# R mixture's scalings from VectorE to GpSimd, and the fourth group's convolution with its matmuls ahead of its casts

## The chip, the cores and the metric

One core of one Trainium2 chip. The time is the device time of one execution, in microseconds (us); a quoted time is the median of several executions. Kernels that are compared ran alternately on the same chip.

## The reference, cut to what matters

`x` is [8, 4160, 192]. First a causal convolution over seven positions with softmax weights for each of 8 heads, then a channel mixture:

```python
x_prev = shift(x, one position)
xk = mu_k * x + (1 - mu_k) * x_prev
xr = mu_r * x + (1 - mu_r) * x_prev
k = maximum(xk @ w_k, 0)              # 192 -> 1024
v = k * k @ w_v                       # 1024 -> 192
out = sigmoid(xr @ w_r) * v
```

## The kernel before

The kernel takes pairs of batches in steps of 512 positions, 34 in all, and writes `xk = x_prev + mu_k * d` with `d = x - x_prev`. A step of ordinary length takes two *rounds* (the code calls them bundles) of TensorE work; each round has 24 K matmuls, 12 R and 32 V, and often some of the convolution of a later group. ScalarE makes relu and sigmoid and the casts of the convolution; VectorE makes the differences, both mixtures, the squares and the product with the sigmoid (`o_sb`). GpSimd issues the loads of x, which cast fp32 to bf16 on the way.

```python
def diff(s, ...):                      # d = y[1:] - y[:-1], three thirds of the channels at once
    nc.vector.tensor_tensor(out=diffs[s], in0=y_of(s, cs, 1), in1=y_of(s, cs, 0), op=ALU.subtract)

def mix(s, i, ...):                    # i = 0: K mixture, i = 1: R mixture
    d = diffs[s]
    t = two.tile([P, NC, STEP], BF16, tag=("xk", "xr")[i])        # two buffers
    ...
    for c in range(sl.start, sl.stop):                            # three scalings of 128x512
        nc.vector.tensor_scalar(out=t[:, c, :L], in0=d[:, c, :L], scalar1=mu[:, i, c : c + 1], ...)
    nc.vector.tensor_tensor(out=o, in0=o, in1=y_of(s, sl, 0), op=ALU.add)
```

The order in which the instructions are written down, for each round `b`:

```python
run(early, b)        # x tile (with a tiny VectorE write into it) and x loads on GpSimd
k_section(ns); k_relu(n) ...; run(rq, b)      # K matmuls, relus, R matmuls
run(vq, b)           # V matmuls
run(mixes, b)        # D round: diff and K mixture of the next step. R round: R mixture
k_square(n) x3; run(vo, b)  # o_sb
run(xt, b); k_square(n); run(late, b)
```

The K, R, V and convolution results share a ring of four PSUM tiles.

## Time and profile before

| | before |
|---|---|
| time | 434.81 us (433.78 to 435.53, 3 runs) |
| TensorE, VectorE, ScalarE, GpSimd busy | 97, 87, 80, 14% |
| a round with and without a convolution | 6.27 and 5.94 us |
| one bf16 scaling of 128x512 on VectorE | 0.35 us |

How to read it: nothing but TensorE is full. What another engine does can cost time only where TensorE comes to wait for it; so one looks not at busy shares but at how late a VectorE result may be before a matmul wants it, and in which of the two rounds.

### The profile page before, as it was taken

The numbers are of one execution on the slowest core, as the hardware profiler recorded it, in microseconds if no ns is written. First come the engines' busy times: TensorE is split into PE (matmuls) and PEld (weight loads), VectorE is DVE, ScalarE is ACT, GpSimd is POOL, SyncE is SP. The second block draws the span as 40 slices with busy tenths as digits, with TensorE's granted clock in tenths as the row PEclk, the third lists the DMA queues.
The fourth block names the chain that finished last, engine by engine and source line by source line (L and its number), as shares of the span: only waits on it lengthen the run. The fifth ranks groups of instructions, "written<-read, shape, count | busy, mean of one in ns | idle before, by whom it ended". The sixth has DMA issues, their size and how long they took to land.

```text
span 433.3 us, 12070 instructions
## 1 busy us (share of the span) xinstructions
PE 419.2 (97%) x5045; PEld 293.3 (68%) x5045; DVE 377.2 (87%) x678; ACT 348.0 (80%) x427; POOL 62.5 (14%) x101
## 2 busy tenths in 40 slices
PE   6879999999999999999999999999999999999995
PEld 3447677667767766776677667766766776667785
DVE  5859978888988899888889989888898889999983
ACT  5776989888988888888889878988898887777780
POOL 6651002123210200303030200203000000000000
PEclk9989999999999999999999999999999999999999
DMA  7998694999996976589796994496847484311223
GB/s 126 192 160 127 166 191 106 195 210 196 193 195 166 177 196 124 87 199 158 181 194 158 175 214 111 96 225 128 185 110 143 119 204 87 111 65 48 74 75 109
DMA packets 136444, 64.73 MB, mean 149 GB/s; under 512 B 87122, under 2 KB 136006, under 8 KB 136390
## 3 DMA queue, kind: packets, MB, share of 16 engines
q1 hardware_dynamic: 96536, 48.29, 47.2%
q0 software_dynamic: 38960, 15.08, 30.2%
q8 instruction: 39, 0.64, 0.6%
q10 hardware_dynamic: 894, 0.61, 0.5%
q14 instruction: 15, 0.12, 0.1%
HBM read 30.75 MB, written 36.96 MB: 156 GB/s over the span
## 4 chain that ended last, share of the span: by engine, by line
PE 90%; ACT 4%; DMA 2%; issue 2%; POOL 1%; DVE 0%; ACTq 0%
PE ps_v L576 41%; PE ps_k L519 38%; PE ps_r L593 7%; PE ps_c L321 4%; ACT k_sb L548 3%; DMA wk<-in_moe_w_k_dram 2%; ACT y L384 1%; POOL xb L155 0%; ACT y L351 0%; PE ps_c L342 0%; PE ps_t L419 0%; ACT r_sb L601 0%; PE ps_c L366 0%; POOL wk L214 0%; DVE x_f L720 0%
## 5 line engine op out<-in xcount | busy, mean ns | idle before, releaser
L548 ACT ACTIVATE k_sb<-ps_k 128x1024 bf16<-128x1024 f32 x260 | 246.1, 1043 | 22.7 <-PE ps_k L519 22.4
L519 PE MATMUL ps_k<-xk,wk 64*128 64x512 bf16 (+1 forms) x1632 | 182.0, 369 | 2.1 <-ACT k_sb L548 1.2
L576 PE MATMUL ps_v<-wv,k 128*128 128x192 bf16 x2080 | 182.7, 246 | 0.9 <-ACT k_sb L548 0.9
L576 PEld LDWEIGHTS <-k 128*128 128x128 bf16 x2080 | 168.7, 98 | 10.9 <-issue 10.9
L562 DVE TENSOR_TENSOR k<-k_sb 128x1024 bf16<-128x1024 bf16 x260 | 167.1, 684 | 0.4 <-ACT k_sb L548 0.4
L519 PEld LDWEIGHTS <-wk 64*128 64x128 bf16 x1632 | 75.0, 94 | 89.1 <-issue 11.4
L617 DVE TENSOR_TENSOR o_sb<-ps_v,r_sb 128x768 f32<-128x768 f32 x64 | 61.2, 956 | 35.5 <-PE ps_v L576 31.7
L384 ACT CAST y<-ps_c 128x960 bf16<-128x960 f32 (+7 forms) x81 | 50.7, 668 | 45.4 <-PE ps_c L321 45.4
L134 POOL DMA_DIRECT2D xb<-in_x_dram x56 | 40.3, 732 | 205.5 <-PE ps_k L519 158.8
L601 ACT ACTIVATE r_sb<-ps_r 128x768 bf16<-128x768 f32 x65 | 55.7, 857 | 1.3 <-PE ps_r L593 1.3
L593 PEld LDWEIGHTS <-xr 64*128 64x128 bf16 x780 | 34.0, 94 | 16.3 <-DVE xb L112 1.3
L593 PE MATMUL ps_r<-wr,xr 64*128 64x192 bf16 x780 | 42.9, 243 | 0.9 <-DVE xb L112 0.8
L499 DVE TENSOR_TENSOR xr<-xr,yT 128x1536 bf16<-128x1536 bf16 (+1 forms) x33 | 31.0, 939 | 1.1
L472 DVE TENSOR_TENSOR d<-yT 128x1536 bf16<-128x1536 bf16 (+2 forms) x35 | 31.1, 887 | 0.8 <-DMA yT<-y_dram 0.7
L499 DVE TENSOR_TENSOR xk<-xk,yT 128x1536 bf16<-128x1536 bf16 (+1 forms) x32 | 30.4, 950 | 1.1
L495 DVE TENSOR_SCALAR xk<-d,mu 128x512 bf16<-128x512 bf16 (+1 forms) x99 | 30.3, 361 | 1.2
L495 DVE TENSOR_SCALAR xr<-d,mu 128x512 bf16<-128x512 bf16 (+1 forms) x102 | 29.3, 343 | 0.0
L321 PE MATMUL ps_c<-xb,toe 64*64 64x240 bf16 (+1 forms) x448 | 20.0, 265 | 0.0
L321 PEld LDWEIGHTS <-toe 64*64 64x64 bf16 x448 | 8.3, 105 | 7.7 <-issue 7.7
L456 POOL COPY y_tail<-yT 128x195 bf16<-128x195 bf16 x4 | 1.6, 398 | 69.6 <-DMA yT<-y_dram 69.6
L428 DVE COPY yT<-ps_t 128x720 bf16<-128x720 bf16 (+1 forms) x7 | 3.2, 500 | 6.7 <-PE ps_t L419 6.7
L131 POOL DMA_DIRECT2D xb<-in_x_dram x14 | 7.6, 544 | 1.4 <-POOL xb L114 0.9
(55 smaller groups left out, 58.5 us busy)
## 6 DMA issues: line engine op xcount, KB each, us to landing
out_dram<-o_sb SPq DMA_DIRECT2D x128, 192.0 KB
xb<-in_x_dram POOLq DMA_DIRECT2D x36, 240.0 KB, 7.3
y_dram<-y SPq DMA_DIRECT2D x22, 360.0 KB
xb<-in_x_dram POOLq DMA_DIRECT2D x10, 216.0 KB, 5.4
y_dram<-y SPq DMA_DIRECT2D x22, 75.0 KB
y_dram<-y SPq DMA_DIRECT2D x6, 216.0 KB
xb<-in_x_dram POOLq DMA_DIRECT2D x6, 144.0 KB, 6.0
xb<-in_x_dram POOLq DMA_DIRECT2D x4, 192.0 KB, 8.0
```

The lines of the kernel that those rows point to most:

```text
L134: nc.gpsimd.dma_start(out=xb[i * Q : (i + 1) * Q, full[0] : full[-1] + 1, s, :], in_=bass.AP(tensor=x.tensor, offset=x.offset + (b * S + b ...
L321: nc.tensor.matmul(out=ps[j * Q : (j + 1) * Q, i, 0 : nb * w].rearrange("p (n s c) -> p n s c", n=nn, s=2)[:, :, :, k * G : (k + 1) * G], ...
L384: copy(out=y[:, :, :, a // Q, :, a % Q : a % Q + b - a], in_=src[:, :, :, :, a - c0 : b - c0])
L495: nc.vector.tensor_scalar(out=t[:, c, :L], in0=d[:, c, :L], scalar1=mu[:, i, c : c + 1], scalar2=None, op0=ALU.mult)
L499: nc.vector.tensor_tensor(out=o, in0=o, in1=y_of(s, sl, 0), op=ALU.add)
L519: nc.tensor.matmul(out=ps[:, i, f * L : (f + 1) * L], lhsT=wk[r, c, fs], rhs=xk[r, c, :L], start=c == 0 and f == 0, stop=c == NC - 1 and f ...
L548: nc.scalar.activation(out=k_sb, in_=ps.rearrange("p a b -> p (a b)"), func=AF.Relu)
L562: nc.vector.tensor_tensor(out=o, in0=i, in1=i, op=ALU.mult)
L576: nc.tensor.matmul(out=o, lhsT=k2s[s][:, f, t * P : (t + 1) * P], rhs=wv[:, f, :], start=(f == 0), stop=(f == NF - 1),)
L593: nc.tensor.matmul(out=ps[:, i, k * D : (k + 1) * D], lhsT=xr[q, c, ts], rhs=wr[q, c, :], start=c == 0, stop=c == NC - 1,)
L601: nc.scalar.activation(out=r_sbs[s, j], in_=ps[:, :, 0 : 2 * D], func=AF.Sigmoid)
L617: nc.vector.tensor_tensor(out=o_sb.rearrange("p (b t) d -> p b (t d)", b=2), in0=v_ps.pop((s, j)), in1=r_sbs.pop((s, j)), op=ALU.mult,)
```

## The change

VectorE is the second busiest engine and GpSimd nearly idle, so from the fourth step on the R mixture's three scalings go there; the add stays. And the fourth group's convolution, whose second bank's matmuls waited for the casts of the first, issues all four matmuls first.

```diff
@@ conv_full
-        for k in range(2):
-            ps = ps2[:, k, 0 : nb * 2 * w].rearrange("p (n s c) -> p n s c", n=nb, s=2)
+        banks = [ps2[:, k, 0 : nb * 2 * w].rearrange("p (n s c) -> p n s c", n=nb, s=2) for k in range(2)]
+        for k, ps in enumerate(banks):
             for i in range(2):
                 ... matmul
+        for k, ps in enumerate(banks):
             ... casts
@@ mix
+        eng = nc.gpsimd if i == 1 and s > 2 else nc.vector
         for c in range(sl.start, sl.stop):
-            nc.vector.tensor_scalar(
+            eng.tensor_scalar(
```

## The prediction

The prediction's time of one GpSimd scaling (0.64 us) and its costs of a collision (0.36 us each; 1.9 to 2.1 us in a D round under the second rival, that of a slower scaling) are my estimates: they rest on rates an element that no run had shown.

> **What bounds the kernel now.** I read the page's busy shares first, then the shares by slice, then the waits that end in a matmul, and last the VectorE and TensorE timelines of one ordinary step.
>
> ```profile
> PE 419.2 (97%) x5045; PEld 293.3 (68%) x5045; DVE 377.2 (87%) x678; ACT 348.0 (80%) x427; POOL 62.5 (14%) x101
> ...
> PE   6879999999999999999999999999999999999995
> ...
> POOL 6651002123210200303030200203000000000000
> ```
>
> TensorE is busy 97% of the span and, after the first 75 us, without a gap that the profile shows. VectorE is at 87%, GpSimd at 14%: that invites the change. But VectorE is not the bound on average; in slices where TensorE is full, freeing VectorE gives nothing by itself.
>
> ```profile
> PE ps_c L342 <- ACT y L351: 2.1, 2, 1.1
> ```
>
> This is the longest entry of TensorE's waits: twice the fourth group's second bank waited for ScalarE's casts of the first. All of TensorE's waits listed there sum to under 10 us, most of it before 25 us.
>
> The VectorE timeline of one step (start, length, instruction; in brackets the idle time before it and what ended it):
>
> ```profile
> 163.74 0.96 DVE L617 TENSOR_TENSOR o_sb<-ps_v,r_sb 128x768 f32<-128x768 f32 x1 [0.79 <-PE ps_v L576]
> 164.62 0.68 DVE L562 TENSOR_TENSOR k<-k_sb 128x1024 bf16<-128x1024 bf16 x1
> 165.22 0.95 DVE L472 TENSOR_TENSOR d<-yT 128x1536 bf16<-128x1536 bf16 x1
> 166.21 0.88 DVE L495 TENSOR_SCALAR xk<-d,mu 128x512 bf16<-128x512 bf16 x3
> 167.12 0.96 DVE L499 TENSOR_TENSOR xk<-xk,yT 128x1536 bf16<-128x1536 bf16 x1
> 168.00 1.89 DVE L562 TENSOR_TENSOR k<-k_sb 128x1024 bf16<-128x1024 bf16 x3
> 170.01 0.96 DVE L617 TENSOR_TENSOR o_sb<-ps_v,r_sb 128x768 f32<-128x768 f32 x1
> 170.88 0.68 DVE L562 TENSOR_TENSOR k<-k_sb 128x1024 bf16<-128x1024 bf16 x1
> 171.48 0.87 DVE L495 TENSOR_SCALAR xr<-d,mu 128x512 bf16<-128x512 bf16 x3
> 172.39 0.96 DVE L499 TENSOR_TENSOR xr<-xr,yT 128x1536 bf16<-128x1536 bf16 x1
> 173.27 1.89 DVE L562 TENSOR_TENSOR k<-k_sb 128x1024 bf16<-128x1024 bf16 x3
> 176.28 0.96 DVE L617 TENSOR_TENSOR o_sb<-ps_v,r_sb 128x768 f32<-128x768 f32 x1 [1.12 <-PE ps_v L576]
> ```
>
> A step is two TensorE rounds of 6.27 us. I call them the D round (o_sb at 163.74 up to the next at 170.01: difference, K scaling) and the R round (170.01 to 176.28, with the three R scalings). The D round is full: from the o_sb at 163.74 nothing idles, and the next one starts 170.01, just as its V matmuls end. The R round has 1.12 us of idle. So VectorE's spare time lies all in the R round, where the scalings are removed, and none in the D round.
>
> ```profile
> 167.16 2.81 PE L576 MATMUL ps_v<-wv,k 128*128 128x192 bf16 x32
> 169.90 0.40 PE L321 MATMUL ps_c<-xb,toe 64*64 64x240 bf16 x8
> 170.24 2.76 PE L519 MATMUL ps_k<-xk,wk 64*128 64x512 bf16 x24
> ```
>
> The PSUM ring has four tiles. The D round's V tile, freed when o_sb ends at 170.97, is taken again four allocations later: a convolution unit, then the third K tile. That K tile starts about half-way in the 24 matmuls, near 171.5. So o_sb may come about 0.57 us later before TensorE waits (about 0.8 us in rounds without a convolution, where the fourth K tile takes it).
>
> [...] The trace of before has one GpSimd operation that reads SBUF beside busy VectorE, the last copy of y_tail:
>
> ```profile
> L456 POOL COPY y_tail<-yT x4: 363/369/493, 107.4 to 370.7; 128x195 bf16<-128x195 bf16 x4
> ```
> ```profile
> 370.32 0.68 DVE L562 TENSOR_TENSOR k<-k_sb 128x1024 bf16<-128x1024 bf16 x1
> 370.92 0.44 DVE L495 TENSOR_SCALAR xr<-d,mu 128x512 bf16<-128x512 bf16 x1
> ```
>
> That copy took 493 ns instead of 363 (it began at 370.72, inside the square), and the scaling behind the square took 0.44 us instead of its usual 0.35. [...] It is one observation, so weak.
>
> **The change part by part.**
>
> *Convolution.* Eight matmuls in two groups of four; the second pair of each no longer waits. It removes at most the 2.1 us of the wait. But ScalarE must still make the same six casts, and a few us later (32 to 37 us) TensorE waits for ScalarE and VectorE (0.23 and 0.37 us). I take half: 1 us gained, once.
>
> *Scalings removed from VectorE.* 31 of the 34 steps, three each: 93 instructions at a pitch of 0.87/3 = 0.29 us, about 27 us of VectorE. They go from the R round, which idled 1.12 us already: idle there becomes about 2 us. On the path: 0.
>
> *Scalings added on GpSimd.* An estimate of one: a copy of 195 elements took 0.363 us[...], together 0.64 us. Three take 1.9 us of a 12.5 us step, and GpSimd has room. The added instruction order shows them released as soon as the difference is written and the R buffer of two steps before is free, not when the R round begins: so they start in the full D round. The add that needs them comes a whole round later, and it won't wait.
>
> *Collision.* The three meet seven VectorE instructions in the D round (three K scalings, add, three squares). What one costs VectorE: the 195-element copy cost about 0.1 us[...], so 0.36 us each, 1.1 us for three. Of that 0.57 us is slack in rounds with a convolution and 0.8 without. Of 31 D rounds 8 have x loads queued on GpSimd just ahead (2.9 us for four), which push the scalings behind most of the round: I count nothing for them. About 15 with a convolution lose 1.1 - 0.57 = 0.53 us each, 8.0 us; about 8 without lose some 0.25 us, 2.0 us. The loss isn't won back: the R round's o_sb waits for the V matmuls that were put off, and the next D round starts from it.
>
> *Sum.* 434.8 - 1 + 10 = 444 us under this theory.
>
> **The rivals.**
>
> [...] If back-to-back VectorE instructions don't let GpSimd in, [...] Nothing stalls, and only the convolution's gain stays: 433 us. Against it speaks the one copy above; for it, that descriptor writing beside squares left nearly all of them at 684 ns[...].
>
> [...] VectorE then loses 1.9 to 2.1 us in the D round: 15 x 1.4 + 8 x 1.2, and some 0.5 in the other 8, is 35 us, near 468 us. Nothing in before's trace shows this operation.
>
> *VectorE relief pays.* If the 27 us counted, the time would fall over 2%. TensorE's gapless rounds of 6.27 us speak against it.
>
> *The x loads come late* behind scalings that wait. The loads run many rounds before their use, so this costs nothing, I think.
>
> **Range and chances.** About half the weight lies on 433 (no collision that shows, or one that fits the slack), a third on 440 to 452, the rest above. I put the point between, at 440 us, and the range at 430 to 461. The limit of 2% is 443.5 us, just where the middle theory lands; so slower by over 2% gets 0.38, within 2% 0.60, and faster 0.02, as no more than some 3 us of removable waiting is to be seen.
>
> **What would show it.** Right, if in the new profile squares and K scalings of VectorE just after a difference are longer than 684 and 346 ns, o_sb of the D round ends over 0.57 us after its V matmuls in excess of before, and K matmuls show waits for o_sb with rounds over 6.27 us. Wrong, if these durations stand as before and TensorE's rounds stay 6.27 us (the first rival), or if one GpSimd scaling's pitch is well over 0.64 us (the second). The convolution is right if the wait for the casts is gone and TensorE is about 1 us ahead at 50 us. All fails if the R add turns out to wait for GpSimd: then my order of release is wrong.

## The result, and the profile after

468.62 us (466.47 to 470.66, 4 runs): slower, with a ratio of 1.0772 (95% interval 1.071 to 1.0834).

From the page of the changed kernel, shares and slices; PEclk is TensorE's granted clock in tenths:

```profile
PE 430.6 (92%) x5045; PEld 301.4 (64%) x5045; DVE 374.2 (80%) x585; ACT 348.5 (74%) x427; POOL 232.0 (50%) x194
...
PE   7789999797798999997799999999599999999996
...
PEclk9989999999799999999799999999899999999999
```

TensorE is no longer gapless: there are three deep dips, near 115, 222 and 335 us, and the clock falls at each (to 7, 7 and 8 tenths in those slices). VectorE's busy time hardly falls (377.2 to 374.2), although 27 us of scalings left it: what remained got longer. GpSimd gained 170 us. The costliest groups show from what:

```profile
L497 POOL TENSOR_SCALAR xr<-d,mu 128x512 bf16<-128x512 bf16 (+1 forms) x93 | 169.4, 1833 | 127.5 <-DVE d L473 84.3
...
L501 DVE TENSOR_TENSOR xr<-xr,yT 128x1536 bf16<-128x1536 bf16 (+1 forms) x33 | 31.4, 952 | 45.4 <-POOL xr L497 45.3
```

One scaling takes 1833 ns on average, not 640, and the R add now waits 45 us for them. The waits say how this gets to TensorE (engine, line, what it waited for: total, times, longest):

```profile
DVE xr L501 <- POOL xr L497: 45.3, 11, 9.8
...
PE ps_k L521 <- ACT k_sb L550: 16.9, 4, 5.8
ACT k_sb L550 <- DVE k L564: 15.5, 3, 5.7
...
PE ps_k L521 <- DVE o_sb L619: 6.7, 12, 1.7
```

The R add stands in VectorE's queue ahead of three squares. While it waits they wait, ScalarE then has no free buffer for its relu, and TensorE no free PSUM tile. One of the three dips, GpSimd's timeline, then VectorE's and TensorE's:

```profile
107.83 0.70 POOL L134 DMA_DIRECT2D xb<-in_x_dram  x1 [12.27 <-issue]
...
110.94 0.71 POOL L134 DMA_DIRECT2D xb<-in_x_dram  x1
111.68 4.65 POOL L497 TENSOR_SCALAR xr<-d,mu 128x512 bf16<-128x512 bf16 x3
```
```profile
100.92 0.95 DVE L473 TENSOR_TENSOR d<-yT 128x1536 bf16<-128x1536 bf16 x1
...
107.22 0.06 DVE L112 MEMSET xb<- 1x1 uint32 x1
116.36 0.96 DVE L501 TENSOR_TENSOR xr<-xr,yT 128x1536 bf16<-128x1536 bf16 x1 [9.09 <-POOL xr L497]
```
```profile
112.21 2.12 PE L521 MATMUL ps_k<-xk,wk 64*128 64x512 bf16 x18
119.10 1.46 PE L521 MATMUL ps_k<-xk,wk 64*128 64x512 bf16 x6 [4.77 <-ACT k_sb L550]
...
121.45 3.65 PE L578 MATMUL ps_v<-wv,k 128*128 128x192 bf16 x32
```

The difference was there at 101.87. GpSimd sat idle before 107.83: next in its queue stood not the scalings but x loads of the same round, and those waited for the tiny VectorE write at 107.22. (So the program has it; the profile's `issue` names no releaser. In all three dips the loads begin 0.6 to 1.3 us after this write.) Then came 3.8 us of loads and 4.65 us of scalings, and the add started at 116.36. After the stall the V matmuls take 3.65 us instead of 2.81: TensorE's clock is 0.50 from 119 to 123 us by the view of stretches.

The distances from one set of V matmuls to the next, kernel against kernel, give a balance, in us. The three dips: 6.05 + 1.89, 7.09 + 1.14, 6.43 + 1.14, together 23.7 (some 0.9 of it in the step of a single round behind the first dip, which experiments 3, 4, 9 and 10 keep). The rounds from each D round with x loads on, three to each: 9.5. A stretch of low clock at 31 us: 1.6. All other rounds together: 1.6. Less 1.7 for an earlier first V, this is 34.8 us before rounding.

Of the 9.5, 1.9 us are not a wait for GpSimd: in one round, at 87 us, the difference waits for the transposing load that brings the convolution's output. Experiment 10, which has that step's scalings back on VectorE, keeps this wait (2.0 us), and experiment 4, with its x loads later, has none. What lengthens it was not tested.

An ordinary D round, VectorE's timeline of the changed kernel:

```profile
181.18 1.31 DVE L497 TENSOR_SCALAR xk<-d,mu 128x512 bf16<-128x512 bf16 x3
...
183.41 2.30 DVE L564 TENSOR_TENSOR k<-k_sb 128x1024 bf16<-128x1024 bf16 x3
185.63 0.95 DVE L619 TENSOR_TENSOR o_sb<-ps_v,r_sb 128x768 f32<-128x768 f32 x1
```

The predicted collision is there: 1.31 instead of 0.88 and 2.30 instead of 1.89, together 0.84 us. But it isn't where most of the 34 us went.

### The profile page after: what moved, and what is told of

It reads as the page before. It is cut to its first block, busy times and chain, and to the rows that moved or that the text cites. A ratio compares the mean times of both kernels' runs of the same rounds, so it can differ in the third digit from the quotient of the medians.

```text
span 468.0 us, 12099 instructions
## 1 busy us (share of the span) xinstructions
PE 430.6 (92%) x5045; PEld 301.4 (64%) x5045; DVE 374.2 (80%) x585; ACT 348.5 (74%) x427; POOL 232.0 (50%) x194
## 5 line engine op out<-in xcount | busy, mean ns | idle before, releaser
L497 POOL TENSOR_SCALAR xr<-d,mu 128x512 bf16<-128x512 bf16 (+1 forms) x93 | 169.4, 1833 | 127.5 <-DVE d L473 84.3
L521 PE MATMUL ps_k<-xk,wk 64*128 64x512 bf16 (+1 forms) x1632 | 187.5, 370 | 26.7 <-ACT k_sb L550 16.9
L578 PE MATMUL ps_v<-wv,k 128*128 128x192 bf16 x2080 | 186.4, 249 | 1.3 <-ACT k_sb L550 1.3
L564 DVE TENSOR_TENSOR k<-k_sb 128x1024 bf16<-128x1024 bf16 x260 | 178.7, 727 | 1.5 <-ACT k_sb L550 1.4
L578 PEld LDWEIGHTS <-k 128*128 128x128 bf16 x2080 | 171.9, 99 | 12.2 <-issue 11.8
L521 PEld LDWEIGHTS <-wk 64*128 64x128 bf16 x1632 | 77.2, 94 | 115.6 <-issue 41.4
L501 DVE TENSOR_TENSOR xr<-xr,yT 128x1536 bf16<-128x1536 bf16 (+1 forms) x33 | 31.4, 952 | 45.4 <-POOL xr L497 45.3
L595 PEld LDWEIGHTS <-xr 64*128 64x128 bf16 x780 | 36.3, 96 | 17.7 <-issue 3.9
L497 DVE TENSOR_SCALAR xk<-d,mu 128x512 bf16<-128x512 bf16 (+1 forms) x99 | 39.5, 454 | 1.2
L501 DVE TENSOR_TENSOR xk<-xk,yT 128x1536 bf16<-128x1536 bf16 (+1 forms) x32 | 32.6, 1018 | 1.1
L715 PE MATMUL warm<-zeros,ones_t 128*128 128x512 bf16 x16 | 6.3, 577 | 1.8 <-DVE zeros L730 1.8
```

Of the source, the lines that this page charges most:

```text
L497: eng.tensor_scalar(out=t[:, c, :L], in0=d[:, c, :L], scalar1=mu[:, i, c : c + 1], scalar2=None, op0=ALU.mult)
L521: nc.tensor.matmul(out=ps[:, i, f * L : (f + 1) * L], lhsT=wk[r, c, fs], rhs=xk[r, c, :L], start=c == 0 and f == 0, stop=c == NC - 1 and f ...
L564: nc.vector.tensor_tensor(out=o, in0=i, in1=i, op=ALU.mult)
L578: nc.tensor.matmul(out=o, lhsT=k2s[s][:, f, t * P : (t + 1) * P], rhs=wv[:, f, :], start=(f == 0), stop=(f == NF - 1),)
L595: nc.tensor.matmul(out=ps[:, i, k * D : (k + 1) * D], lhsT=xr[q, c, ts], rhs=wr[q, c, :], start=c == 0, stop=c == NC - 1,)
```

## The experiments

The first theory is that of the **queue**: GpSimd's scalings take so long, and stand behind x loads in so many steps, that the R add waits. The second is the prediction's, that of the **collision**: in each D round VectorE loses time to the GpSimd scalings that run beside it (the 0.84 us just seen). Each diff is against the changed kernel, unless it says otherwise.

**1. The convolution alone.**

```diff
-        eng = nc.gpsimd if i == 1 and s > 2 else nc.vector
+        eng = nc.vector
```

> The convolution part alone, all scalings on VectorE. The prediction took half of the 2.1 us wait as gain: 1 us faster than before, 434 us. Rival, from the trace of the changed kernel, where TensorE is 1.7 us ahead at 31 us but only 0.1 us ahead at 40 us: the gain is given back within one round, and the time is that of before to within 0.3 us.

433.95 us against 434.86, ratio 0.9978 (0.9951 to 1.0006): the same within 2%. The medians show a gain of 0.9 us; by the interval it may be anything from 2.1 us faster to 0.3 us slower. TensorE in its trace, then in that of the kernel before:

```profile
23.46 0.98 PE L342 MATMUL ps_c<-xb,toe 128*128 128x240 bf16 x8
24.45 2.79 PE L521 MATMUL ps_k<-xk,wk 64*128 64x512 bf16 x24
28.37 0.67 PE L595 MATMUL ps_r<-wr,xr 64*128 64x192 bf16 x12 [1.12 <-ACT k_sb L550]
```
```profile
27.18 4.07 PE L519 MATMUL ps_k<-xk,wk 64*128 64x512 bf16 x24
```

All eight convolution matmuls run in one piece, and TensorE is 1.75 us ahead at the second V (38.41 against 40.16). Little of this is the wait itself: its 2.1 us are gone, but waits of 1.12, 0.24 and 0.60 us for ScalarE come behind the K matmuls, where before there was one of 0.23. Most is clock: in the kernel before a stretch of low clock (0.61 and 0.54 in the four us from 26 on) follows the two waits, and its K matmuls take 4.07 us instead of 2.79. Five of the six traces with the old order show such a stretch there; the sixth (experiment 7, second V at 39.02) has none, and the lead over it is 0.6 us. Of the seven with the new order one has it, the changed kernel, and later. No run holds the clock fixed, so what the order gains by itself isn't settled.

Of these 1.75 us, 1.06 goes again in one later round, where the difference waits 0.94 us for a transposing load. The rival, that all is lost within one round, was read from the changed kernel's trace and fell: there a stretch of half clock fell into those V matmuls, here none did.

**2. The scalings alone.** The second part of the diff put on the kernel before.

> The scalings on GpSimd alone, the convolution as before. If the whole loss is the scalings': 468 to 469 us, as the changed kernel. If the convolution part had a share in the loss, clearly less than 468.

470.24 us (466.82 to 473.16), ratio 1.0803. The loss is the scalings'.

**3. The scalings ahead of the loads.** They are written down right after the difference; the add stays in the R round.

```diff
+    def scale_r(s):
+        xrs[s] = two.tile([P, NC, STEP], BF16, tag="xr", name="xr")
+        scale(s, 1, xrs[s])          # the three scalings, as before
         at(mixes, fb - 1, diff, s)
+        if s > 2:
+            at(mixes, fb - 1, scale_r, s)
```

> The three scalings are emitted right after the difference, so that GpSimd has them ahead of the x loads that wait for the R round; the add stays where it was. Theory of the queue (the loss is GpSimd's order: scalings behind loads that wait): the three stalls of 7.6 to 8.2 us go, 469 - 24 = 445 us, and the R add no longer waits 9 us anywhere, only about 2 to 3 us in the 8 rounds whose loads come in the D round. Theory of the collision[...]: nothing changes, 466 to 471 us.

447.63 us, ratio 1.0292 (1.0258 to 1.0327). Not one instruction fewer is on GpSimd or VectorE, and 21 of the 34 us are back. The R add's waits fall from 45.3 to 17.4 us, 3.1 the longest, and TensorE's granted clock is 0.997 on average. The collision alone can't explain that.

```profile
DVE xr L510 <- POOL xr L481: 17.4, 8, 3.1
```

**4. The loads behind them too.** As 3, and the loads are written down at the end of their round.

```diff
-            at(early, b, load_x, g)
+            at(late, b, load_x, g)
```

> As the run before, and the x loads are emitted at the end of their round, so that no load stands ahead of a scaling of the same step. Theory of the queue: no R add waits for GpSimd; what is left is collisions, 0.13 to 0.23 us a step in the changed kernel's undisturbed rounds, times 28 steps: about 5 us, 438 to 441 us. Theory of the collision: still over 460 us.

438.06 us, ratio 1.0072 (1.0041 to 1.0104). The R add waits 2.1 us in all, most of it in the step of one round. What is left is mostly collision: 23 rounds are longer by 0.12 to 0.17 us, 3.2 us together. Three others are longer by 0.88 (the step of one round), 0.57 and 0.32 us, and against all this stands a first V that is 1.6 us earlier. One of its R rounds, VectorE:

```profile
173.08 0.96 DVE L510 TENSOR_TENSOR xr<-xr,yT 128x1536 bf16<-128x1536 bf16 x1
173.96 1.89 DVE L573 TENSOR_TENSOR k<-k_sb 128x1024 bf16<-128x1024 bf16 x3
177.29 0.96 DVE L628 TENSOR_TENSOR o_sb<-ps_v,r_sb 128x768 f32<-128x768 f32 x1 [1.44 <-PE ps_v L587]
```

This is the room that the change was to make, and it ends as 1.44 us of VectorE's waiting for TensorE. Even well ordered the change is slower than the kernel before, by 0.4 to 1.0%.

**5. Decoys in the D round.** A decoy is work whose result nobody uses. The kernel before; GpSimd scales the difference into a tile that nobody reads.

```diff
+    def decoy(s):
+        t = two.tile([P, NC, STEP], BF16, tag="decoy", name="decoy")
+        for c in range(NC):
+            nc.gpsimd.tensor_scalar(out=t[:, c, :L], in0=diffs[s][:, c, :L], scalar1=mu[:, 1, c : c + 1], ...)
         at(mixes, fb - 1, diff, s)
+        if s > 2:
+            at(mixes, fb - 1, decoy, s)
```

> The kernel before, its own scalings on VectorE, and three GpSimd scalings of the difference into a scratch tile that nobody waits for, at the place in the D round where the moved ones run. This is collision without the queue. Theory of the queue: a few us, 437 to 442 us, with K scalings and squares of VectorE stretched by about 0.4 us twice a step. Theory of the collision: 455 us or more. [...]

441.77 us, ratio 1.0162 (1.0126 to 1.0197). So a bare collision costs some 7 us when VectorE keeps its own scalings besides. The first rival falls, for VectorE's times don't stand as before: its K scalings went from 366 to 466 ns on average, its squares from 684 to 735.

**6. Decoys in the R round.** The same, held back by a VectorE write of two elements at the start of the R round.

```diff
+        nc.vector.memset(t[0:1, 0, 0:2], 0.0)      # in decoy, ahead of the scalings
-            at(mixes, fb - 1, decoy, s)
+            at(mixes, last_bundle[s] - (s < LAST), decoy, s)
```

> The same decoys, held back by a small VectorE write until the R round, where VectorE idles 0.8 to 1.1 us. If the slack of the round decides what a collision costs: 435 to 437 us, less than the decoys of the D round by 2 us or more, though as many VectorE instructions are stretched. If collisions cost alike anywhere: the same time as the decoys of the D round.

437.75 us, ratio 1.0067 (1.0031 to 1.0104): a little above the expected, and 4 us below the decoys of the D round. Squares are as long (727 ns), R scalings 468 instead of 349. Its R round, VectorE:

```profile
173.73 1.04 DVE L495 TENSOR_SCALAR xr<-d,mu 128x512 bf16<-128x512 bf16 x2
...
175.68 2.30 DVE L571 TENSOR_TENSOR k<-k_sb 128x1024 bf16<-128x1024 bf16 x3
178.25 0.96 DVE L626 TENSOR_TENSOR o_sb<-ps_v,r_sb 128x768 f32<-128x768 f32 x1 [0.26 <-PE ps_v L585]
```

The same 2.30 us for three squares, and `o_sb` still waits for TensorE. All rounds but three keep their length from before; these three come right behind the R rounds with x loads and carry 2.2 us of the loss, and 0.6 us were lost before the first decoy ran. A collision costs what the round it falls in can't spare.

**7. Decoys that only write.** As 5, but with memsets of 1740 elements behind a tiny VectorE write; they are about as long.

```diff
-            nc.gpsimd.tensor_scalar(out=t[:, c, :L], in0=diffs[s][:, c, :L], ...)
+            nc.gpsimd.memset(t, 0.0)
```

> The same place in the D round, but three GpSimd memsets of 1740 elements, of about the same length (estimate from 0.42 us for 384 elements: 1.55 us each), which write and don't read. If only GpSimd's reads hold up squares and adds: these keep 684 and 962 ns, K scalings alone stretch, and the time is 435 to 437 us. If any GpSimd access does: as the reading decoys.

527.21 us (523.50 without the one slow run of the four, 535.65), ratio 1.2099: far off. Squares and adds did stay at 683 and 964 ns, as expected. But a K scaling met by a memset of 1.55 us took 1.74 us and ended 0.15 us after it, VectorE and GpSimd:

```profile
174.33 1.74 DVE L495 TENSOR_SCALAR xk<-d,mu 128x512 bf16<-128x512 bf16 x1
```
```profile
174.37 1.55 POOL L506 MEMSET decoy<- 128x1740 bf16 x1 [5.63 <-DVE decoy L504]
```

K scalings took 1297 ns on average. I had taken it that GpSimd instructions of the same length hold VectorE up alike. An estimate puts both in one picture: memsets of 384 elements (the shortest in the kernel before) and of 1740 took 418 and 1568 ns, 0.85 ns an element; 512 elements at that rate are 0.43 us, which is what a GpSimd scaling of 1.55 us holds VectorE up. VectorE would then be held up for the elements moved and not for the instruction's length. These figures agree with this; no run tests it.

**8. The cost by itself.** After the last VectorE work of the kernel before, GpSimd alone.

```diff
+        for n in (128, 256, 384, 512):
+            for _ in range(3):
+                nc.gpsimd.tensor_scalar(out=dst[:, 0:n], in0=src[:, 0:n], scalar1=mu[:, 1, 0:1], ...)
+        ...                                       # a constant factor, copies, fp32
```

> After the last VectorE work of the kernel before, GpSimd alone makes scalings of 128, 256, 384 and 512 bf16 elements by a per-partition factor, then 512 by a constant, copies of 512, and scalings of 256 fp32 elements. The prediction's estimate: [...]0.64 us at 512. From the changed kernel's undisturbed scalings (1.55 us at 512, 0.92 at 256): about 0.3 us + 2.5 ns an element. If the per-partition factor is what costs, the constant one takes about 0.64 us; if it is the arithmetic, the copy alone does.

One look (its total of 458.18 us includes the measured part, so it isn't compared; a single run's state is unknown). Groups of that stretch:

```profile
L767 POOL TENSOR_SCALAR dst<-src,mu 128x512 bf16<-128x512 bf16 x3 | 4.7, 1562 | 0.3
L769 POOL TENSOR_SCALAR dst<-src 128x512 bf16<-128x512 bf16 x3 | 4.5, 1489 | 0.3
...
L767 POOL TENSOR_SCALAR dst<-src,mu 128x256 bf16<-128x256 bf16 x3 | 2.8, 922 | 0.3
...
L771 POOL COPY dst<-src 128x512 bf16<-128x512 bf16 x3 | 1.8, 612 | 0.2
```

The copy of 512 takes 612 ns, close to my 640, and with the 363 ns of 195 elements that is 0.79 ns an element. The scaling takes 2.5 ns an element ((1562 - 922)/256; 603 and 1242 ns at 128 and 384 elements fit) and 0.28 us fixed; 256 fp32 elements took 922 ns too. It is the arithmetic that costs, for a constant factor saves only 5% (1489 ns) and a copy has none.

**9. Three steps back on VectorE,** those whose R round begins with x loads.

```diff
-        eng = nc.gpsimd if i == 1 and s > 2 else nc.vector
+        load_at = {13, 28, 44}
+        eng = nc.gpsimd if i == 1 and s > 2 and last_bundle[s] - 1 not in load_at else nc.vector
```

> The changed kernel, but in the 3 of 31 steps whose R round begins with x loads on GpSimd the scalings go back to VectorE; nothing else moves. Theory of the queue: those 3 steps carry the three long stalls (7.9, 8.2 and 7.6 us), so taking 3 of 31 steps back recovers some 24 us, 445 us. If the loss were spread over the steps by collisions or by GpSimd's slowness: 34 x 3/31, about 3 us, 465 us.

445.19 us, ratio 1.023 (1.0188 to 1.0272). 3 of 31 steps carried 23 us.

**10. All 11 steps with loads back on VectorE.** The same set with the rounds 8, 10, 15, 19, 25, 31, 35 and 41, tested against the step's D round as well as its R round.

> The same for all 11 steps with x loads in their D or R round; 20 steps keep their scalings on GpSimd. Theory of the queue: as with the loads moved late, only collisions stay, 0.13 us in 18 to 20 rounds, 2 to 3 us, less the convolution's gain of 0.9: 436 to 438 us, and no R add waits for GpSimd except in the step of one round.

437.96 us, ratio 1.008 (1.0038 to 1.0122), as with the loads moved (438.06). Two different ways of keeping loads and scalings apart end at nearly the same time. That they agree to 0.1 us is chance: this one has fewer collisions but loses 1.8 us in the round with the wait for a transposing load.

**11. One scaling on GpSimd, two on VectorE.**

```diff
-            eng.tensor_scalar(
+            (nc.gpsimd if i == 1 and s > 2 and c == 0 else nc.vector).tensor_scalar(
```

> The changed kernel with one of the three scalings on GpSimd and two on VectorE. GpSimd's chain is 1.55 instead of 4.65 us, so a scaling behind the loads of an R round ends 3.1 us sooner and is still some 5 us late (4 us of loads, 1.55 of scaling, less what VectorE does meanwhile): each of the three stalls falls from about 8 to 3 or 4 us, the add waits of 1.9 to 3.1 us go, and one collision a step (0.43 us) fits the slack of 0.57 us: 443 to 448 us. If the collisions were the loss, a third of it would stay, 446 us, but spread over all rounds; so it is the rounds' lengths that tell, 6.27 us in the ordinary ones by the first theory.

449.93 us, ratio 1.035 (1.0303 to 1.0398), 2 us above the expected. The ordinary rounds are 6.27 us, as in the kernel before: one collision fits the slack. The three dips are 3.8, 4.6 and 3.8 us, and the add waits 5.5, 6.2 and 5.5 us. A third of the work keeps nearly half of the loss, for the loads (3.8 us in the changed kernel's first dip) still stand ahead.

No version beats the kernel before beyond doubt; the convolution alone is the only one that may.

## Why the prediction was wrong

The range ended at 461 us, and the time was 468.6. By its own steps:

- **What bounds the kernel**: right. TensorE's rounds set the time, and VectorE's spare time lay in the R round. The 27 us taken from VectorE gained nothing (experiment 4).
- **Convolution, 1 us**: not settled; 0.9 us in the medians with an interval that includes none. The reason given, that ScalarE must still make the casts, came true: the 2.1 us went, and waits for ScalarE of 1.96 us stood in their place. What put TensorE 1.75 us ahead was mostly the clock, which the prediction didn't have, and 1.06 us of that went again at a transposing load. So the size is near by luck.
- **"Scalings added on GpSimd": the step that failed**, in both halves. The 0.64 us were worked out from a copy and a rate that no run had shown. They are near the 612 ns of a copy; a scaling takes 1.55 us with nothing in its way (experiment 8), three of them 4.65 us and in a busy D round 5.80. And "they start in the full D round. The add that needs them comes a whole round later, and it won't wait" held in 20 of 31 steps: in 11 the add waited. One of these is the step of a single round; in the other 10 x loads stand ahead in GpSimd's queue, and in 3 of those the loads wait for a VectorE write of the R round itself. I had read the waits of the scalings, but not those of the instruction ahead of them: GpSimd kept its order, and scalings whose input was there at 101.87 us began at 111.68.
- **"I count nothing for them"**, for the 8 steps with loads in the D round: the rounds from these on cost 9.5 us, 1.9 of it the wait for a transposing load. The loads of the three R rounds weren't counted at all: 23.7 us, two thirds of the loss; experiments 3 and 9 recover 21 and 23 us. Part of it is the low clock after a stall: 0.50, 0.50 and 0.60 in the four us from 119, 224 and 334 on, 1.00 in the same stretches of the kernel before.
- **Collision**: right in kind, too large. I took 0.36 us for each of three collisions and so 0.53 us of stall; measured are 0.43 and 0.41 us, in two. The third scaling, from 185.42 us on, ran beside `o_sb` and a square, which took 0.95 and 0.68 us as in the kernel before (0.96 and 0.68). The slack was also 0.12 us larger than I said: squares ended at 169.89 and `o_sb` began at 170.01. 0.84 - 0.57 - 0.12 = 0.15 us, and the rounds of experiment 4 show 0.12 to 0.17. So 3 us in place of 10. (The 0.57 is itself loose: 171.5 - 170.97 is 0.53, and the middle of the K matmuls by its own line is 171.62, which gives 0.65.)
- **The rivals**: the second, a scaling slower than 0.64 us, named 468 us and is right in number but not in way. It had VectorE lose 1.9 to 2.1 us in the D round, from a rate that was not shown; measured are 0.84, and a scaling of 1.55 us held VectorE up by 0.43. Slowness cost through the queue. The first fell (experiment 5). "The x loads come late" asked whether the scalings delay the loads; it was the loads that delayed the scalings.
- **What would show it**: "All fails if the R add turns out to wait for GpSimd". That is the line which came true.

## What to carry to other kernels

Before work goes to an idle engine, read that engine's whole queue: here the scalings came only after 3.8 us of loads written down ahead of them, and those waited for the very engine that was to be relieved (its write at 107.22 us, in the first dip). Price the operation itself on the new engine, not one that looks like it (1.56 us for a scaling of 512 elements, 0.61 for a copy). And look for the slack in each place: the 27 us taken off VectorE where it had slack gained nothing (ratio 1.0072 in experiment 4), while the collisions cost 0.12 to 0.17 us in each of 23 rounds.
